# An attention and MLP block: output products over three PSUM banks, scale factors made in PSUM, epsilon as an activation's bias

## The chip, the cores and the metric

The kernel runs on one core of a Trainium2 chip. The metric is the device time of one execution in microseconds (us). Before the change it was 2750.64 us, the median of three runs (2748.8 to 2751.75). Five engines run side by side, each through its own list of instructions in order: TensorE (PE in the profile, its weight loads PEld), VectorE (DVE), ScalarE (ACT), GpSimd (POOL) and SyncE (SP), which issues most of the transfers. Work is held back by semaphores, that is by waits for the end of an instruction on another engine or of a transfer.

## The reference

The input `x` has 2048 rows of 576 values. A condition vector gives shifts, gains and gates; 32 query heads share 16 key and value heads of 512 keys each; the MLP is 4608 wide.

```python
mod = (_silu(c) @ w_mod).reshape(c.shape[0], 6, 1, -1)
sa, ca, ga, sb, cb, gb = (mod[:, 0], mod[:, 1], mod[:, 2], mod[:, 3], mod[:, 4], mod[:, 5])
h = _layernorm(x, axis=-1) * (1 + ca) + sa
x = x + ga * _A_ref(h, A_k_cache, A_v_cache, A_wq, A_wo)
h = _layernorm(x, axis=-1) * (1 + cb) + sb
x = x + gb * _B_ref(h, B_w1, B_w3, B_w2)
```

`_A_ref` projects to queries, takes scores against the last 512 cached keys, a softmax, the sum over the values and an output product with `wo` (4096 by 576). `_B_ref` is `(silu(h @ w1) * (h @ w3)) @ w2`.

## The kernel before

**Tiling.** The rows go in four blocks `b` of 512, each of four row tiles `t` of 128. Every matrix is held as a high and a low half in float16, so that a product is three matmuls: high by high, high by low, low by high. The scale factors that make the halves fit are powers of two, worked out on the chip from the largest value of each matrix.

**Slots and steps.** The attention runs in 128 slots, one for each head and row block, each of four steps t = 0 to 3. The order of every engine's work is the order of the program. In a step TensorE does, in this order: at t = 1 four transposes of probabilities into a T bank (`turn`, L548); the scores of tile t (L513, three matmuls of 512 columns); for t < 3 a part of the next slot's query (L440, L444); one call of `attend_out` (L615); and what the lists of tasks hold for that step. At the end of a slot come the twelve matmuls of `values` (L593). VectorE takes the largest score (L517), ScalarE the exponential `p` (L531) and its high half (L563), GpSimd the low half (L568), and SyncE transposes them by DMA into `ptw` (L575).

**Output products.** For two heads (a pair) and one row tile, a unit, the product with `wo` is twelve matmuls of 128 by 288: two heads, three products of halves, two column halves. A unit is two calls of `attend_out`, j = 0 at an even step and j = 1 at the next, odd one, six matmuls each (L463), written by `back` into the two banks of one tile `E`. After the second, VectorE adds the unit, scaled, to `acc` (L623). The first call of pair p is in slot 2p + 4 at t = 2. `lane` alternates between `E` and a second tile `pf` only from slot n = 128 on, when the T banks are given up for it (L1628).

**PSUM.** Eight banks: two named A (queries and values), two S (scores), two in the tile `E`, two T, each of one bank. T holds the turned probabilities, and also the turned rows of `make_h` (L1446, blocks 2 and 3 of the attention's input, read by `modulate`, L261) and of `store_h` (L655, blocks 0 and 1 of the MLP's input), which have five turns m = 0 to 4, one for each 128 columns, at t = m mod 3. `E` serves a few others: columns 400 to 416 of its second bank take the sums of `sum_peaks` (L330), columns 408 to 411 those of the MLP's weights (`in_total`, `out_total`), and the whole tile the gate rows of `mod_rows` (L176) and the first query (L489).

**Scale steps.** `sum_peaks` spreads the largest values of a weight group over all partitions by a small matmul (L333); `take_sums` (L335) copies them to SBUF (L338); at a later step `scales` (L349) turns them into powers of two by `powers` (L315: L318, L319 and a reciprocal, L320) and for queries and keys into three pairs of factors (`score_factors`, L342, with L345). Queries, keys and values come four to a step (columns 0 to 4), the output's one alone (column 4). `total` tasks run inside `attend_out`, ahead of the accumulation, `taken` tasks behind it, and the step's other tasks after these.

**Norm.** `norm_root` (L210) adds epsilon on VectorE (L213 or L215) and takes the root on ScalarE (L216).

**Start.** The first block's rows are turned into T, T, A, A and S banks, the first query goes to the first bank of `E` (`project_first`, L447 to L456), and `make_h(1)` runs in the first two slots with `early`.

Of the kernel before, what the change touches and what calls it, by code (L numbers as in the profile page):

```python
# [48 lines left out]
def tile_block(  # L49
# [30 lines left out]

    E = psum.tile([P, 2, 512], F32, tag="E", name="pe", bufs=1)
    turning = ExitStack()
    tpool = turning.enter_context(tc.tile_pool(name="tpool", bufs=2, space=PSUM))

    def t_bank():
        return tpool.tile([P, 512], F32, tag="T", name="pt")

# [73 lines left out]
    def mod_cols(wm, name, one, tag):  # L161

        ps = t_bank() if tag == "T" else bank(tag, f"ps_{name}")
# [12 lines left out]
    def mod_rows(wm, kind):  # L176

        vec = gate_rows[kind]
        wm = wm[0]
        for h in range(2):  # L180
            for d in (0, 3):
                nc.tensor.matmul(
                    E[:, h, :HALF], ones, wm[:, d, h * HALF : (h + 1) * HALF], start=d == 0, stop=d == 3
                )
        nc.vector.tensor_copy(half_split(vec), E[:, :, :HALF])
        return vec
# [23 lines left out]
    def norm_root(b):  # L210
        rstd = norms[b][0][:, :, 1]
        if ("out", b) in norms:
            nc.vector.tensor_scalar(rstd, rstd, 1.0 / D, EPS, op0=ALU.mult, op1=ALU.add)  # L213
        else:
            nc.vector.tensor_scalar(rstd, rstd, EPS, None, op0=ALU.add)  # L215
        nc.scalar.activation(rstd, rstd, AF.Sqrt)  # L216

# [36 lines left out]
    def turn_rows(b, m, tag):  # L254

        ps = t_bank() if tag == "T" else bank(tag, "ps_n")
        for t in range(ST):
            nc.tensor.transpose(ps[:, t * P : (t + 1) * P], norms[b][1][t][:, m * P : (m + 1) * P], ident)  # L258
        return ps
# [70 lines left out]
    def sum_peaks(g, lo, hi, ps=None):  # L330

        ps = E[:, 1, 400:416] if ps is None else ps
        nc.tensor.matmul(ps[:, lo:hi], peak_ones, tops[g][:, lo:hi], start=True, stop=True)  # L333

    def take_sums(g, lo, hi, ps=None):  # L335

        ps = E[:, 1, 400:416] if ps is None else ps
        nc.vector.tensor_copy(peaks[g][:, 5 + lo : 5 + hi], ps[:, lo:hi])  # L338

    def score_factors(g):  # L340
        for at_, small, by in (
            (0, peaks[g][:, 5:10], score_down), (3, peaks[g][:, 5:10], turned_down),  # L342
            (5, peaks[g][:, 10:15], log_up),
        ):
            nc.vector.tensor_scalar(  # L345
                factors[:, g, at_ : at_ + 2], small[:, 0:2], small[:, 2:3], by, op0=ALU.mult, op1=ALU.mult
            )

    def scales(g, lo, hi):  # L349

        small = peaks[g]
        powers(small, small[:, 5:10], lo, hi, 5, 2.0**-14)
        down = small[:, 5:10]
        if lo == 0:
            score_factors(g)
        elif lo == 4:
            nc.vector.tensor_scalar(
                factors[:, g, 2:3], down[:, 4:5], down[:, 3:4], gate_down, op0=ALU.mult, op1=ALU.mult
            )
# [97 lines left out]

    def back(ps, o, w, t, first, last):

        rows = slice(t * P, (t + 1) * P)  # L460
        for n, (x, y) in enumerate(((0, 0), (0, 1), (1, 0))):
            for h in range(2):
                nc.tensor.matmul(  # L463
                    ps[:, h, :HALF],
                    o[:, x, rows],
                    w[:, y, h * HALF : (h + 1) * HALF],
                    start=first and n == 0,
                    stop=last and n == 2,
                )

    QP = (range(0, 5), range(5, 10), range(10, 14))
# [13 lines left out]
    def query(i, part):  # L485
        u, j, b = slots[i]
        st = state[i]
        if part == 0 or i == 0:
            st["q"] = bank("A", "pq") if i else E[:, 0, :]  # L489
        ps = st["q"]  # L490
        if i == 0:
            project_first(ps, wqs[u, j], hT[b])
        else:
            project(ps, wqs[u, j], hT[b], QP[part])
        if part == len(QP) - 1:
            q = st["qT"] = pool.tile([P, 2, SB], F16, tag=("qh", "ql")[i % 2], name="qT", bufs=QB)
            nc.scalar.activation(q[:, 0], ps, AF.Copy, scale=Q_DOWN)
            if not i:
                query_low(i)
# [48 lines left out]
    def turn(i, t):  # L548

        st = state[i]  # L550
        p = st.pop(("p", t))
        ps = st["t"] = t_bank().rearrange("p (j n) -> p j n", j=KC)
        for j in range(KC):
# [60 lines left out]

    def attend_out(pair, t, j, total):  # L615
        u, _, b = slots[2 * pair]
        lane[0] += j == 0
        ps = spare()
        back(ps, state[2 * pair + j]["o"], wos[u][:, j], t, j == 0, j == 1)
        if j == 1:  # L620
            run(*total)
            a = half_split(acc[b][:, t, :])
            nc.vector.scalar_tensor_tensor(  # L623
                a, ps[:, :, :HALF], factors[:, uses[u][0], 2:3], a, op0=ALU.mult, op1=ALU.add
            )
# [29 lines left out]
    def store_h(b, m, tag, tag_out):  # L655
# [8 lines left out]
        )  # L664
        store_later(hd[b][m * P : m * P + n, :], hf[:n], ("s", b, m) if tag == "T" else None)

# [266 lines left out]
    def down(d, u):  # L933

        pair = d // G
        lane[0] += 1
        ps = lane[1][lane[0] % 2]
        if u < 4:
# [28 lines left out]
    def plain(j, i, t):  # L967

        d = 2 * G - 1
        lane[0] += 1  # L970
        ps = lane[1][lane[0] % 2]
        w = osets[d, 3 if j else 4]
# [181 lines left out]

    lane = [0, ()]

    def spare():
        return lane[1][lane[0] % 2] if lane[1] else E

    def in_peak(f, part):  # L1160
# [8 lines left out]
    def in_total(f):  # L1169

        m = peak_cols[:, 4 * (f % 2) :][:, :4]
        for part in range(2):
            peak = m[:, 2 * part + 1 : 2 * part + 2]
            nc.tensor.matmul(
                spare()[:, 1, 408:410], peak.to_broadcast([P, P]), m[:, 2 * part : 2 * part + 2],
                start=part == 0, stop=part == 1,
            )

    def in_taken(f):
        nc.vector.tensor_copy(stats[:, f, :], spare()[:, 1, 408:410])  # L1180

# [23 lines left out]
    def out_total(p):  # L1205
        nc.tensor.matmul(spare()[:, 1, 410:411], peak_ones, peak_cols[:, 8 + p % 2 : 9 + p % 2], start=True, stop=True)

    def out_taken(p):
        nc.vector.tensor_copy(out_down[:, p : p + 1], spare()[:, 1, 410:411])

# [235 lines left out]
    def make_h(b, m, early=False):  # L1446
        modulate(hT[b], m, turn_rows(b, m, "T"), vecs["shift", "a"], vecs["gain", "a"], early)

# [33 lines left out]
    for b, i in ((0, 111), (1, 114)):  # L1482
        norm(i, b)
        for m in range(DC + 1):
            at(i + 1 + m // 3, m % 3, store_h, b, m, "T", "raw")
            step_at(ST * (i + 1 + m // 3) + m % 3 + 1, store_now, ("s", b, m))
# [43 lines left out]
    for i, k in ((13, 5), (105, 3), (108, 4)):  # L1530
        at(i - 1, -1, load, wms, k, load_mod, k)
        for d in range(DC + 1):
            at(i, min(d, ST - 1), weigh, k, d)
    at(14, 1, make_gate, "b", 5)
    at(14, 2, lambda: scale_gate("b", mlp_small, mlp_gate_down))
    at(106, 2, make_cols, "shift", "b", 3, 0.0, "T")
    at(109, 2, make_cols, "gain", "b", 4, 1.0, "T")
    at(109, 3, lambda: spread_peaks("b", mlp_small))
    at(110, 1, lambda: scale_cols("b", t_bank(), mlp_small, 2.0**-8))
    for piece in range(6):  # L1540
# [21 lines left out]
    for t in (0, 2, 1, 3):  # L1562
        norm_rows(0, t)
    turned = [turn_rows(0, m, "TTAAS"[m]) for m in range(DC + 1)]
    for m in range(DC + 1):
        weigh_col(wms[0], 0, m, m < 2)
    for k, key in enumerate((wqs[0, 0], wqs[0, 1], keys[0])):
        find_peak(0, k, key)
    sum_peaks(0, 0, 3)
    junk = bank("S", "ps_warm")  # L1570
    warm(junk, WARM[0])
    take_sums(0, 0, 3)
    powers(peaks[0], peaks[0][:, 5:10], 0, 3, 5, 2.0**-14)
    raws = [wqs[0, j] for j in range(2)]
# [12 lines left out]
    modulate_first(hT[0], turned, vecs["shift", "a"], vecs["gain", "a"])  # L1587
    score_factors(0)
    keys[0] = split_k_low(*keys[0], 0)
# [143 lines left out]
```

## Time and profile before

| | |
|---|---|
| time, median of three runs | 2750.64 us |
| lowest and highest | 2748.80, 2751.75 us |
| the profiled execution | 2750.74 us |
| its span, first to last instruction | 2748.9 us |
| TensorE busy | 2678.7 us, 97% |
| VectorE busy | 1943.0 us, 71% |
| ScalarE busy | 1622.0 us, 59% |
| GpSimd busy | 1874.0 us, 68% |
| moved by DMA | 463.87 MB, 169 GB/s |

The page gives busy time per engine; a group row gives an operation's line, the tiles it writes and reads, its count, its busy time and mean, and then the idle time of its engine just before it with what ended that. A row of the timeline is a start in microseconds, a duration, the engine and line, and in square brackets the idle time ahead of it and what ended it. A row of waits reads: engine, tile, line, what it waited for; the sum in microseconds, how often, and the longest. A row of one source line gives the shortest, the middle and the longest duration in ns. Attention fills the span to about 1616 us, the MLP the rest.

### The profile page before, as it was taken

The page shows a single profiled execution, that of the slowest core. Times are in us where ns is not written, and L with a number is a line of the kernel's source. Part 1 is how long each engine was busy: PE and PEld are TensorE (multiplying, and loading weights), DVE is VectorE, ACT ScalarE, POOL GpSimd, SP SyncE. Part 2 cuts the span into 40 slices and gives each one's busy share as a digit, 9 for nine tenths or more (in the row PEclk, how much of TensorE's full clock was granted, in tenths as well). Part 3 has the DMA queues.
Part 4 walks back from the last instruction along what each step waited for, and adds up shares of the span by engine and source line. Part 5 has one row for each costly group of instructions (what it writes and reads, how often), then busy time and mean ns, then how long its engine had stood idle before and what let it go on. Part 6 is the DMA issues. An engine that isn't in the chain of part 4 may idle for free. (4 is left out here: it accounts for less than half of the span.)

```text
span 2748.9 us, 45218 instructions
## 1 busy us (share of the span) xinstructions
PE 2678.7 (97%) x15406; PEld 1510.3 (55%) x15406; DVE 1943.0 (71%) x3582; ACT 1622.0 (59%) x3026; POOL 1874.0 (68%) x1747
## 2 busy tenths in 40 slices
PE   6899999999999999999999999999999999999998
PEld 3455555555555555555555555555555555555555
DVE  7876777777777777877765567777776666566566
ACT  6776778777777778787677635544443333333332
POOL 4677888888888877877669536688874455333435
PEclk9999999999999999999999999999999999999999
DMA  6888888788787878879879945656643444333332
GB/s 200 184 175 196 184 182 186 176 188 187 167 181 170 190 186 211 200 179 212 187 192 226 224 137 169 201 168 200 209 151 111 153 122 128 106 102 112 104 109 81
DMA packets 593463, 463.87 MB, mean 169 GB/s; under 512 B 442704, under 2 KB 472528, under 8 KB 592208
## 3 DMA queue, kind: packets, MB, share of 16 engines
q1 hardware_dynamic: 592944, 460.69, 66.1%
q8 instruction: 121, 1.98, 0.3%
q14 instruction: 110, 0.90, 0.1%
q10 hardware_dynamic: 288, 0.30, 0.0%
HBM read 264.19 MB, written 95.99 MB: 131 GB/s over the span
## 5 line engine op out<-in xcount | busy, mean ns | idle before, releaser
L568 POOL TENSOR_TENSOR hp<-p,hp 128x512 f16<-128x512 f32 x384 | 447.6, 1168 | 267.0 <-ACT hp L563 154.5
L531 ACT ACTIVATE p<-pss,table,factors 128x512 f32<-128x512 f32 x512 | 396.8, 775 | 351.2 <-DVE table L517 182.4
L517 DVE CUSTOM_DVE_ANT_0 spent<-pss,factors 128x512 uint8<-128x512 f32 x512 | 381.2, 745 | 237.6 <-PE pss L513 236.2
L880 PEld LDWEIGHTS <-wset 128*128 128x128 f16 x3528 | 344.2, 98 | 337.2 <-issue 3.7
L880 PE MATMUL py<-hset,wset 128*128 128x512 f16 x2016 | 482.1, 379 | 0.0
L463 PE MATMUL pe<-o 128*128 128x288 f16 x3024 | 453.0, 286 | 10.6 <-DVE acc L623 10.3
L513 PE MATMUL pss<-k,qT 128*128 128x512 f16 x1536 | 417.7, 380 | 15.3 <-ACT p L531 13.0
L463 PEld LDWEIGHTS <-o 128*128 128x128 f16 x3072 | 300.4, 98 | 184.8 <-issue 16.3
L593 PE MATMUL po<-ptw,v 128*128 128x512 f16 x1536 | 357.1, 381 | 8.8 <-DMA ptw<-hp 2.7
L880 PE MATMUL px<-hset,wset 128*128 128x512 f16 x1512 | 361.5, 379 | 2.2 <-ACT p L531 2.2
L94 POOL TENSOR_TENSOR akv<-u,akv 128x512 f16<-128x512 f32 x141 | 165.2, 1181 | 178.0 <-ACT akv L93 170.2
L440 PE MATMUL pq<-hT,wq 128*128 128x512 f16 x1092 | 280.5, 379 | 0.0
L563 ACT CAST hp<-p 128x512 f16<-128x512 f32 x384 | 237.4, 618 | 15.5 <-DMA ptw<-hp 2.3
L593 PEld LDWEIGHTS <-v 128*128 128x128 f16 x1536 | 147.6, 98 | 174.6 <-issue 13.0
L513 PEld LDWEIGHTS <-qT 128*128 128x128 f16 x1536 | 147.3, 98 | 129.3 <-issue 17.4
L965 PEld LDWEIGHTS <-akv 128*128 128x128 f16 x1728 | 169.0, 98 | 89.3 <-issue 0.7
L623 DVE SCALAR_TENSOR_TENSOR acc<-pe,factors,acc 128x576 f32<-128x576 f32 x252 | 204.2, 810 | 13.0 <-PE pe L463 5.1
L613 POOL TENSOR_TENSOR o<-on,o 128x512 f16<-128x512 f32 x128 | 149.7, 1170 | 54.6 <-ACT o L612 52.2
L440 PEld LDWEIGHTS <-wq 128*128 128x128 f16 x1092 | 106.9, 98 | 127.2 <-issue 1.0
L959 DVE SCALAR_TENSOR_TENSOR acc<-pf,table,acc 128x576 f32<-128x576 f32 x140 | 113.5, 811 | 79.3 <-PE pf L965 79.3
L1058 ACT COPY u<-py 128x512 f32<-128x512 f32 x72 | 42.2, 586 | 200.8 <-PE py L880 198.8
L1051 ACT ACTIVATE s<-s,table 128x512 f32<-128x512 f32 x72 | 52.0, 722 | 175.6 <-DVE s L1050 175.6
(254 smaller groups left out, 4734.2 us busy)
## 6 DMA issues: line engine op xcount, KB each, us to landing
wset<-wd SPq DMA_DIRECT2D x213, 320.0 KB, 3.2
r<-row SPq DMA_DIRECT2D x128, 256.0 KB, 3.9
oset<-od SPq DMA_DIRECT2D x106, 288.0 KB, 3.2
wraw<-in_w SPq DMA_DIRECT2D x36, 768.0 KB, 5.4
wd<-wmade SPq DMA_DIRECT2D x75, 320.0 KB, 3.5
wset<-wd SPq DMA_DIRECT2D x71, 160.0 KB, 2.2
w2raw<-in_w SPq DMA_DIRECT2D x19, 576.0 KB, 5.2
wd<-ring SPq DMA_DIRECT2D x33, 320.0 KB, 2.7
```

What stands on the lines that cost most here:

```text
L94: eng.tensor_sub(halves[:, 1], src, halves[:, 0])
L440: nc.tensor.matmul(ps, w[:, k // 2, m, :], hT[:, DC + m if k == 1 else m, :], start=s == 0, stop=False)
L463: nc.tensor.matmul(ps[:, h, :HALF], o[:, x, rows], w[:, y, h * HALF : (h + 1) * HALF], start=first and n == 0, stop=last and n == 2,)
L513: nc.tensor.matmul(pss, q[:, x, rows], k[:, y, :], start=n == 0, stop=n == 2)
L517: nc.vector.tensor_tensor_reduce(spent, pss, to_log.to_broadcast([P, W]), turned, 3.0e38, op0=ALU.add, op1=ALU.min, accum_out=nm)
L531: nc.scalar.activation(p, pss, AF.Exp, bias=nm, scale=factor, accum_out=st["l"][:, t : t + 1])
L563: nc.scalar.copy(hp[:, 0, :], state[i]["p", t])
L568: nc.gpsimd.tensor_sub(hp[:, 1, :], state[i].pop(("p", t)), hp[:, 0, :])
L593: nc.tensor.matmul(po, v[:, x, c, :], pt[:, y, c, :], start=c == 0 and n == 0, stop=c == KC - 1 and n == 2)
L623: nc.vector.scalar_tensor_tensor(a, ps[:, :, :HALF], factors[:, uses[u][0], 2:3], a, op0=ALU.mult, op1=ALU.add)
L880: nc.tensor.matmul(ps, w[:, a, :], h[:, b, :], start=start and n == 0, stop=stop and n == 6, skip_group_check=True)
L965: nc.tensor.matmul(ps[:, h, :HALF], a[:, rows], w[:, b, :], start=m == 0, stop=m == 2)
```

## The change

`E` becomes one tile of three banks, in the pool that held the T banks, and T has one bank. `lane` flips with every unit: a unit takes the middle bank and one outer bank, first or last. Part 0 (the even step) issues six terms into the outer bank, part 1 (the odd step) the six terms for the middle bank; for t = 0 the last term of part 0 is put off to part 1. `idle()` is the outer bank that the running unit does not use: turned rows, column vectors and gates go there. The sums go to columns 400 and up of the third bank, where `take_sums` now works out the powers in place and copies both columns to SBUF once; `score_factors` reads them there. Epsilon is the bias of the root's activation. `make_gate` "b" and its scaling move one step later. The first sums are taken in an S bank, the first rows are turned into `E[:, 0]` and `E[:, 1]`, the first query goes to `E[:, 2]`, and the early `make_h(1)` alternates between `E[:, 0]` and `E[:, 1]`. At slot n the pool is closed and two tiles of two banks, `pe` and `pf`, are allocated.

```diff
-    E = psum.tile([P, 2, 512], F32, tag="E", name="pe", bufs=1)
-    tpool = turning.enter_context(tc.tile_pool(name="tpool", bufs=2, space=PSUM))
-    def t_bank():
-        return tpool.tile([P, 512], F32, tag="T", name="pt")
+    tpool = turning.enter_context(tc.tile_pool(name="tpool", bufs=1, space=PSUM))
+    E = tpool.tile([P, 3, 512], F32, tag="E", name="pe")
+    lane = [1, ()]
+    def both_halves():
+        banks = lane[1][lane[0]] if lane[1] else E[:, lane[0] : lane[0] + 2]
+        return banks[:, :, :HALF]
+    def idle():
+        return E[:, 2 - 2 * lane[0], :]
+    def spare():
+        return lane[1][lane[0]][:, 1] if lane[1] else E[:, 2]
...
-        if ("out", b) in norms:
-            nc.vector.tensor_scalar(rstd, rstd, 1.0 / D, EPS, op0=ALU.mult, op1=ALU.add)
-        else:
-            nc.vector.tensor_scalar(rstd, rstd, EPS, None, op0=ALU.add)
-        nc.scalar.activation(rstd, rstd, AF.Sqrt)
+        nc.scalar.activation(rstd, rstd, AF.Sqrt, bias=eps_col, scale=1.0 / D if ("out", b) in norms else 1.0)
...
-        ps = t_bank() if tag == "T" else bank(tag, "ps_n")
+        ps = idle() if tag == "E" else E[:, int(tag), :] if tag in "012" else bank(tag, "ps_n")
...
-        nc.vector.tensor_copy(peaks[g][:, 5 + lo : 5 + hi], ps[:, lo:hi])
+        both = ps[:, :10].rearrange("p (k n) -> p k n", n=5)[:, :, lo:hi]
+        d, up = both[:, 0], both[:, 1]
+        nc.vector.tensor_scalar(d.bitcast(I32), d.bitcast(I32), EXPONENT, None, op0=ALU.bitwise_and)
+        nc.vector.tensor_scalar(d, d, 2.0**-40, 2.0**-14, op0=ALU.max, op1=ALU.mult)
+        nc.vector.reciprocal(up, d)
+        nc.vector.tensor_copy(peaks[g][:, 5:15].rearrange("p (k n) -> p k n", n=5)[:, :, lo:hi], both)
+    def score_factors(g, ps=None):
+        ps = E[:, 2, 400:416] if ps is None else ps
+        for at_, k, by in ((0, 0, score_down), (3, 0, turned_down), (5, 5, log_up)):
             nc.vector.tensor_scalar(
-                factors[:, g, at_ : at_ + 2], small[:, 0:2], small[:, 2:3], by, op0=ALU.mult, op1=ALU.mult
+                factors[:, g, at_ : at_ + 2], ps[:, k : k + 2], peaks[g][:, k + 7 : k + 8], by,
+                op0=ALU.mult, op1=ALU.mult,
...
     def scales(g, lo, hi):
-        small = peaks[g]
-        powers(small, small[:, 5:10], lo, hi, 5, 2.0**-14)
-        down = small[:, 5:10]
+        down = peaks[g][:, 5:10]
...
-            st["q"] = bank("A", "pq") if i else E[:, 0, :]
+            st["q"] = bank("A", "pq") if i else E[:, 2, :]
...
-        ps = st["t"] = t_bank().rearrange("p (j n) -> p j n", j=KC)
+        ps = st["t"] = tpool.tile([P, KC, P], F32, tag="T", name="pt")
...
-    def attend_out(pair, t, j, total):
-        lane[0] += j == 0
-        ps = spare()
-        back(ps, state[2 * pair + j]["o"], wos[u][:, j], t, j == 0, j == 1)
-        if j == 1:
+    TERMS = tuple((j, x, y) for j in range(2) for x, y in ((0, 0), (0, 1), (1, 0)))
+    def attend_out(pair, t, part, total):
+        if not part:
+            lane[0] = 1 - lane[0]
+        now, last = lane[0], [(lane[0], TERMS[-1])] if t == 0 else []
+        if part:
+            jobs = last + [(1 - now, term) for term in TERMS]
+        else:
+            jobs = [(now, term) for term in TERMS[: len(TERMS) - len(last)]]
+        for h, (j, x, y) in jobs:
+            nc.tensor.matmul(
+                both_halves()[:, h],
+                state[2 * pair + j]["o"][:, x, t * P : (t + 1) * P],
+                wos[u][:, j, y, h * HALF : (h + 1) * HALF],
+                start=(j, x, y) == TERMS[0],
+                stop=(j, x, y) == TERMS[-1],
+            )
+        if part:
...
-    at(14, 1, make_gate, "b", 5)
-    at(14, 2, lambda: scale_gate("b", mlp_small, mlp_gate_down))
+    at(14, 2, make_gate, "b", 5)
+    at(14, 3, lambda: scale_gate("b", mlp_small, mlp_gate_down))
...
-    at(110, 1, lambda: scale_cols("b", t_bank(), mlp_small, 2.0**-8))
+    at(110, 1, lambda: scale_cols("b", idle(), mlp_small, 2.0**-8))
...
-    turned = [turn_rows(0, m, "TTAAS"[m]) for m in range(DC + 1)]
+    turned = [turn_rows(0, m, "01AAS"[m]) for m in range(DC + 1)]
...
-                    lane[1] = (E, after.tile([P, 2, 512], F32, tag="T2", name="pf"))
+                    lane[1] = tuple(after.tile([P, 2, 512], F32, tag=tag, name=tag) for tag in ("pe", "pf"))
```

More of the change, by code (lines that the diff above doesn't have):

```diff
@@ L142, in tile_block @@
     ones = ones.to_broadcast([P, P])
+    eps_col = const.tile([P, 1], F32, name="eps_col")
+    nc.gpsimd.memset(eps_col, EPS)
     peak_cols = const.tile([P, 12], BF16, name="peak_cols")
@@ L161, in mod_cols @@
     def mod_cols(wm, name, one, tag):
-        ps = t_bank() if tag == "T" else bank(tag, f"ps_{name}")
+        ps = idle() if tag == "E" else bank(tag, f"ps_{name}")
         wm = wm[0]
@@ L179, in mod_rows @@
         wm = wm[0]
+        ps = E[:, 1 - lane[0] : 3 - lane[0], :HALF]
         for h in range(2):
@@ L182, in mod_rows @@
                 nc.tensor.matmul(
-                    E[:, h, :HALF], ones, wm[:, d, h * HALF : (h + 1) * HALF], start=d == 0, stop=d == 3
+                    ps[:, h], ones, wm[:, d, h * HALF : (h + 1) * HALF], start=d == 0, stop=d == 3
                 )
-        nc.vector.tensor_copy(half_split(vec), E[:, :, :HALF])
+        nc.vector.tensor_copy(half_split(vec), ps)
         return vec
@@ L330, in sum_peaks @@
     def sum_peaks(g, lo, hi, ps=None):
-        ps = E[:, 1, 400:416] if ps is None else ps
+        ps = E[:, 2, 400:416] if ps is None else ps
         nc.tensor.matmul(ps[:, lo:hi], peak_ones, tops[g][:, lo:hi], start=True, stop=True)
     def take_sums(g, lo, hi, ps=None):
[L337 to L344, printed above, removed]
+        ps = E[:, 2, 400:416] if ps is None else ps
+        both = ps[:, :10].rearrange("p (k n) -> p k n", n=5)[:, :, lo:hi]
[5 more added lines that the diff above has]
+    def score_factors(g, ps=None):
+        ps = E[:, 2, 400:416] if ps is None else ps
+        for at_, k, by in ((0, 0, score_down), (3, 0, turned_down), (5, 5, log_up)):
             nc.vector.tensor_scalar(
-                factors[:, g, at_ : at_ + 2], small[:, 0:2], small[:, 2:3], by, op0=ALU.mult, op1=ALU.mult
+                factors[:, g, at_ : at_ + 2], ps[:, k : k + 2], peaks[g][:, k + 7 : k + 8], by,
+                op0=ALU.mult, op1=ALU.mult,
             )
     def scales(g, lo, hi):
-        small = peaks[g]
-        powers(small, small[:, 5:10], lo, hi, 5, 2.0**-14)
-        down = small[:, 5:10]
+        down = peaks[g][:, 5:10]
         if lo == 0:
@@ L456, in project_first @@
                     nc.tensor.matmul(ps, w[:, k, DC, :], hT[:, 2 * DC, :], start=False, stop=False)
[L458 to L469, printed above, removed]
     QP = (range(0, 5), range(5, 10), range(10, 14))
@@ L623, in attend_out @@
             nc.vector.scalar_tensor_tensor(
-                a, ps[:, :, :HALF], factors[:, uses[u][0], 2:3], a, op0=ALU.mult, op1=ALU.add
+                a, both_halves(), factors[:, uses[u][0], 2:3], a, op0=ALU.mult, op1=ALU.add
             )
@@ L664, in store_h @@
         )
-        store_later(hd[b][m * P : m * P + n, :], hf[:n], ("s", b, m) if tag == "T" else None)
+        store_later(hd[b][m * P : m * P + n, :], hf[:n], ("s", b, m) if tag == "E" else None)
     def combine_tiles(pair):
@@ L935, in down @@
         pair = d // G
-        lane[0] += 1
-        ps = lane[1][lane[0] % 2]
+        lane[0] = 1 - lane[0]
+        ps = lane[1][lane[0]]
         if u < 4:
@@ L969, in plain @@
         d = 2 * G - 1
-        lane[0] += 1
-        ps = lane[1][lane[0] % 2]
+        lane[0] = 1 - lane[0]
+        ps = lane[1][lane[0]]
         w = osets[d, 3 if j else 4]
@@ L1153, in tile_block @@
     nc.gpsimd.memset(odd_cols, 1.0)
-    lane = [0, ()]
-    def spare():
-        return lane[1][lane[0] % 2] if lane[1] else E
     def in_peak(f, part):
@@ L1174, in in_total @@
             nc.tensor.matmul(
-                spare()[:, 1, 408:410], peak.to_broadcast([P, P]), m[:, 2 * part : 2 * part + 2],
+                spare()[:, 412:414], peak.to_broadcast([P, P]), m[:, 2 * part : 2 * part + 2],
                 start=part == 0, stop=part == 1,
@@ L1179, in in_taken @@
     def in_taken(f):
-        nc.vector.tensor_copy(stats[:, f, :], spare()[:, 1, 408:410])
+        nc.vector.tensor_copy(stats[:, f, :], spare()[:, 412:414])
     def power_of(up, d, down):
@@ L1205, in out_total @@
     def out_total(p):
-        nc.tensor.matmul(spare()[:, 1, 410:411], peak_ones, peak_cols[:, 8 + p % 2 : 9 + p % 2], start=True, stop=True)
+        nc.tensor.matmul(spare()[:, 414:415], peak_ones, peak_cols[:, 8 + p % 2 : 9 + p % 2], start=True, stop=True)
     def out_taken(p):
-        nc.vector.tensor_copy(out_down[:, p : p + 1], spare()[:, 1, 410:411])
+        nc.vector.tensor_copy(out_down[:, p : p + 1], spare()[:, 414:415])
     def out_scale(p):
@@ L1446, in make_h @@
     def make_h(b, m, early=False):
-        modulate(hT[b], m, turn_rows(b, m, "T"), vecs["shift", "a"], vecs["gain", "a"], early)
+        modulate(hT[b], m, turn_rows(b, m, str(m % 2) if early else "E"), vecs["shift", "a"], vecs["gain", "a"], early)
     def statistics(i, b, steps):
@@ L1484, in tile_block @@
         for m in range(DC + 1):
-            at(i + 1 + m // 3, m % 3, store_h, b, m, "T", "raw")
+            at(i + 1 + m // 3, m % 3, store_h, b, m, "E", "raw")
             step_at(ST * (i + 1 + m // 3) + m % 3 + 1, store_now, ("s", b, m))
@@ L1533, in tile_block @@
             at(i, min(d, ST - 1), weigh, k, d)
-    at(14, 1, make_gate, "b", 5)
-    at(14, 2, lambda: scale_gate("b", mlp_small, mlp_gate_down))
-    at(106, 2, make_cols, "shift", "b", 3, 0.0, "T")
-    at(109, 2, make_cols, "gain", "b", 4, 1.0, "T")
+    at(14, 2, make_gate, "b", 5)
+    at(14, 3, lambda: scale_gate("b", mlp_small, mlp_gate_down))
+    at(106, 2, make_cols, "shift", "b", 3, 0.0, "E")
+    at(109, 2, make_cols, "gain", "b", 4, 1.0, "E")
     at(109, 3, lambda: spread_peaks("b", mlp_small))
-    at(110, 1, lambda: scale_cols("b", t_bank(), mlp_small, 2.0**-8))
+    at(110, 1, lambda: scale_cols("b", idle(), mlp_small, 2.0**-8))
     for piece in range(6):
@@ L1568, in tile_block @@
         find_peak(0, k, key)
-    sum_peaks(0, 0, 3)
     junk = bank("S", "ps_warm")
+    first_sums = junk[:, 400:416]
+    sum_peaks(0, 0, 3, first_sums)
     warm(junk, WARM[0])
-    take_sums(0, 0, 3)
-    powers(peaks[0], peaks[0][:, 5:10], 0, 3, 5, 2.0**-14)
+    take_sums(0, 0, 3, first_sums)
     raws = [wqs[0, j] for j in range(2)]
@@ L1587, in tile_block @@
     modulate_first(hT[0], turned, vecs["shift", "a"], vecs["gain", "a"])
-    score_factors(0)
+    score_factors(0, first_sums)
     keys[0] = split_k_low(*keys[0], 0)
```

## The prediction

> **What bounds the kernel.** I read the head of the page, the cores view, the groups of instructions by line on TensorE, then its waits by releaser.
>
> ```profile
> PE 2678.7 (97%) x15406; PEld 1510.3 (55%) x15406; DVE 1943.0 (71%) x3582; ACT 1622.0 (59%) x3026; POOL 1874.0 (68%) x1747
> core 0: 2748.9 us, clock 0.997
> L463 PE MATMUL pe<-o 128*128 128x288 f16 x3024 | 453.0, 286 | 10.6 <-DVE acc L623 10.3 <-DVE us L338 0.2
> L513 PE MATMUL pss<-k,qT 128*128 128x512 f16 x1536 | 417.7, 380 | 15.3 <-ACT p L531 13.0 <-ACT qT L497 0.9 <-DVE qT L503 0.5
> PE pss L513 <- ACT p L531: 13.0, 17, 2.4
> PE pe L463 <- DVE acc L623: 10.3, 14, 2.0
> ```
>
> TensorE is busy 97% of the span at a granted clock of 0.997, and its order is fixed, so time moves only where TensorE itself waits. 2748.9 − 2678.7 leaves 70 us of idle time in all; the two waits above, 23.3 us, are those at which the change is near. The sum is made against the profiled execution, 2750.74 us (span 2748.9 and 1.8 around it); the median of the runs, 2750.64, is the same to 0.1. A measurement tells about 0.2%, 5.5 us, from no change.
>
> The output products keep their 12 matmuls a unit, and their order is free of cost: 453.0 us over 3024 is 150 ns each, whichever bank comes next. So the change is priced in waits alone.
>
> **What it removes: long scale operations.** The factor steps are tiny VectorE operations on SBUF.
>
> ```profile
> L319 DVE TENSOR_SCALAR us<-us x35: 153/155/1349, 16.1 to 1259.8; 128x1 f32<-128x1 f32 x19, 128x4 f32<-128x4 f32 x15, 128x3 f32<-128x3 f32 x1
> L345 DVE TENSOR_SCALAR factors<-us,sc x48: 257/282/1448, 29.3 to 1216.3; 128x2 f32<-128x2 f32 x48
> L338 DVE COPY us<-pe x33: 145/151/161, 14.8 to 1255.3; 128x1 f32<-128x1 f32 x17, 128x4 f32<-128x4 f32 x15, 128x3 f32<-128x3 f32 x1
> L345 DVE TENSOR_SCALAR factors<-us,sc 128x2 f32<-128x2 f32 x48 | 23.4, 546 | 0.0
> L319 DVE TENSOR_SCALAR us<-us 128x1 f32<-128x1 f32 (+2 forms) x35 | 14.8, 423 | 1.2
> L318 DVE TENSOR_SCALAR us<-us 128x1 int32<-128x1 int32 (+2 forms) x35 | 9.3, 266 | 0.5
> 400.81 1.40 POOL L846 TENSOR_TENSOR w2raw<-w2raw,gate_b 128x576 f32<-128x576 f32 x1
> 400.89 1.35 DVE L319 TENSOR_SCALAR us<-us 128x4 f32<-128x4 f32 x1
> 402.17 1.16 POOL L568 TENSOR_TENSOR hp<-p,hp 128x512 f16<-128x512 f32 x1
> 402.37 0.98 DVE L345 TENSOR_SCALAR factors<-us,sc 128x2 f32<-128x2 f32 x1
> 407.49 0.81 PE L513 MATMUL pss<-k,qT 128*128 128x512 f16 x3 [1.05 <-ACT p L531]
> 410.40 0.81 PE L513 MATMUL pss<-k,qT 128*128 128x512 f16 x3 [0.45 <-ACT p L531]
> 313.69 0.81 PE L513 MATMUL pss<-k,qT 128*128 128x512 f16 x3 [1.21 <-ACT p L531]
> 115.52 0.90 PE L463 MATMUL pe<-o 128*128 128x288 f16 x6 [0.30 <-DVE acc L623]
> 599.43 0.77 PE L463 MATMUL pe<-o 128*128 128x288 f16 x5 [0.29 <-DVE acc L623]
> ```
>
> At 400.89 a 155 ns operation takes 1349 ns and ends at 402.24, when GpSimd's L846 ends (402.21). Over the mean-minus-shortest of each group, 48 × 0.289 + 35 × 0.270 + 35 × 0.13 is 28 us of VectorE time lost beside GpSimd. L338, the one with its source in PSUM, never exceeds 161 ns. [...]
>
> What that is worth is not 28 us but what TensorE later waits: 6 to 10 us behind each such step, ScalarE is late with `p` and scores wait (407.49: 1.05, 410.40: 0.45; 313.69: 1.21). Followed step by step over the 12 late score factors from 109 to 1166 us, with 0.1 to 0.2 us more of restart per wait than the idle figure shows, these give 11.2 us; the wait total of L513 on p, 13.0, less three in the first 90 us, bounds it above with the accumulator waits of the same steps (115.5: 0.3, 599.4: 0.3). The dropped value-factor operations add 0.5. Gain **11.7** (bounds 8 and 14).
>
> ```profile
> 8.49 0.17 DVE L215 TENSOR_SCALAR mv<-mv 128x4 f32<-128x4 f32 x1
> 214.60 1.72 PE L182 MATMUL pe<-wm,ones 128*128 128x288 f32 x6 [0.91 <-DVE acc L623]
> ```
>
> Epsilon as a bias removes L215; only the first, 0.17 us at 8.49, lies ahead of TensorE's first work: gain 0.2. `make_gate` "b" moves from t = 1, behind a running accumulation, to t = 2, where none runs: its 0.91 (1.07 with the restart) falls away, and part 1 of that unit waits about 0.3 for its copy: gain 0.8. Together the gains are **12.7 us**.
>
> **What it adds: waits of the one tile.** Does TensorE, writing one bank of E, wait for readers of another?
>
> ```profile
> 730.54 0.15 DVE L338 COPY us<-pe 128x1 f32<-128x1 f32 x1
> 730.74 0.77 PE L463 MATMUL pe<-o 128*128 128x288 f16 x5 [0.21 <-DVE us L338]
> PE pe L463 <- DVE us L338: 0.2, 1, 0.2
> ```
>
> The first matmul at 730.74 writes bank 0 (`h` 0); L338 reads columns 400 to 416 of bank 1. It waits all the same, to 0.05 us after the copy. So E is ordered as a whole, and the change keeps E one tile, of three banks. Two things follow. Part 0 of a unit still waits for the accumulation of the last one although its own bank is free: the 10.3 us of L463 on acc stay, but for the 0.6 counted above. And what used to go to the two T banks, the transposes of `make_h` and `store_h`, now waits for whatever reads E.
>
> ```profile
> 138.89 0.90 PE L463 MATMUL pe<-o 128*128 128x288 f16 x6
> 139.62 0.60 PE L258 MATMUL pt<-ident,xn 128*128 128x128 f32 x4
> 139.82 0.82 DVE L623 SCALAR_TENSOR_TENSOR acc<-pe,factors,acc 128x576 f32<-128x576 f32 x1
> 140.06 0.81 PE L513 MATMUL pss<-k,qT 128*128 128x512 f16 x3
> 143.39 0.90 PE L463 MATMUL pe<-o 128*128 128x288 f16 x6
> 144.18 0.77 ACT L273 ACTIVATE hf<-pt,mod_a 128x512 f32<-128x512 f32 x1
> ```
>
> Terms, each a delay of TensorE, with all its queue behind the waiting instruction:
> - Transposes at t = 1 (m = 1 and 4 of two `make_h` and two `store_h` blocks: eight) come right behind part 1. They start at 139.62; the accumulation ends at 140.64. 140.64 + 0.06 − 139.62 = 1.08; eight are 8.6. One of them also stands behind a value sum (0.7), and one lets the next part 0 wait (0.3): **9.7**. Scores are queued behind it, and VectorE and ScalarE behind those, which had little ahead; nothing hides it.
> - Transposes at t = 2 (m = 2, four) are read by ScalarE's modulation, 144.95 its end, while part 1 wants E at 143.39: 1.56, and 1.4 to 2.2 at the other three. TensorE is already 1.08 late there in part, so I take **4.1** (3.1 to 7.4). Those at t = 0 leave part 1 some 0.1 to 1 us behind their read: nothing.
> - `scale_cols` in the idle bank, one more wait for an accumulation: **1.1**.
>
> ```profile
> 102.89 0.14 DVE L338 COPY us<-pe 128x1 f32<-128x1 f32 x1
> 103.45 0.78 PE L463 MATMUL pe<-o 128*128 128x288 f16 x5
> ```
>
> - `take_sums` becomes four operations in PSUM. For a single value sum it stands at t = 1, and part 0 comes 103.45 − 103.03 = 0.42 after the copy. Three more operations at 0.15 to 0.2 start to start (400.50 to 400.69 to 400.89) are 0.6: 0.2 late at each of 15: **3.2** (0 to 7, if such operations in PSUM take 0.1 or 0.3). At the fours (t = 3) seven operations, 1.35 us, face 0.9 to 2.0 of room: **0.9**.
>
> ```profile
> 23.61 2.12 PE L450 MATMUL pe<-hT,wq 128*128 128x512 f16 x8 [0.74 <-ACT hT L287]
> 25.45 0.79 ACT L287 ACTIVATE hf<-pt,mod_a 128x512 f32<-128x512 f32 x1
> 28.91 0.92 PE L453 MATMUL pe<-hT,wq 128*128 128x512 f16 x3 [0.76 <-POOL hT L296]
> 38.43 0.63 PE L258 MATMUL pt<-ident,xn 128*128 128x128 f32 x4 [0.79 <-DVE hT L269]
> 41.80 1.11 PE L258 MATMUL pt<-ident,xn 128*128 128x128 f32 x4 [2.74 <-ACT hT L271]
> ```
>
> - Prologue. The first rows turned stand in E, and the first query too: it must wait for the last read of them, 26.24, in place of 23.61. The end of that query hangs on GpSimd's low part (28.91) in any case, so of 2.6 I take 0.9 (0 to 2.4). The early `make_h(1)` had two T banks in turn; in E its five turns go one after another with their reads: the third, at 41.80, moves to about 44.15, **+2.3**. Prologue **3.2** (0.5 to 6).
>
> Costed at nothing: the single bank for T's `turn`, used once a step, its copies out done a step ahead; part 0 now needs the second head's `o` a step earlier, and has 4 us of room; the pool renewed at slot n; no DMA is moved.
>
> **Sum:** 9.7 + 4.1 + 1.1 + 3.2 + 0.9 + 3.2 = 22.2 lost, 12.7 gained, **+9.5: 2760 us**. With the upper and lower ends of the unsure terms, its own range is 2750 to 2770.
>
> **Rivals.**
> - **E is ordered bank by bank (faster).** Place: part 0's first matmul, and the t = 1 transposes. If only readers of the same bank hold TensorE, the outer bank is free while VectorE adds up the last unit, and the idle bank while it is read.
>
> ```profile
> 1535.18 0.90 PE L463 MATMUL pe<-o 128*128 128x288 f16 x6 [1.99 <-DVE acc L623]
> ```
>
>   Such waits as 1535.18 then go: of the 10.3 some 5 find nothing else late behind them, and with the slower matmuls that follow 1535 and the restarts 8.4. The locks bring 11.2, gate and epsilon 0.6 or more; the idle bank still costs 3.4 where its read comes into part 0, and the chains 1. 2750.7 − 8.4 − 11.2 − 0.6 + 3.4 + 1.0 ≈ **2735**. It decides from the point that a matmul starts in E while the accumulation of the unit before runs. The row at 730.74 speaks against it. [...] Chance 0.12.
> - **The added waits are half hidden (no change).** Time lost at 139 to 192 us may be got back at later waits for GpSimd or DMAs, as TensorE still has 70 us of idle time; then 22 becomes about 12, and the time is **2750**. Against it: those waits are rare between 135 and 300 us. Chance 0.25.
> - **The locks stay, or the reads run at their upper ends (slower still).** Each scale operation also takes a scalar or the copy's target from SBUF; if the long ones remain, 2760 + 11 ≈ **2771**. L338, whose target lies in SBUF, speaks against it. Chance 0.08.
> - **Forecast:** 0.55.
>
> **How the numbers follow.** Likeliest is the forecast, 2760. Leaving out most of the fast rival (0.12) and the top of the slow one, the range is 2743 to 2772. Faster by over 5.5 us: the fast rival and a tail, 0.13. Within 5.5: the hidden case, 0.25. Slower: 0.62.
>
> **What would show it.** Right: L318, L319 and L345's successors all under 0.3 us; the waits of L513 on p down from 13.0 to about 3; L463 on acc still near 10; new waits of the transposes on acc near 1 us, eight times, and of L463 on ScalarE's modulation. Wrong: part 0 starting while the accumulation before it runs, or transposes with no wait at 139 and 1387 us, would mean the fast rival; scale operations over 1 us, the slow one.

## The result and the profile after

The changed kernel takes 2766.16 us (median of 6 runs, 2765.08 to 2774.07) beside 2750.21 us for the kernel before: a ratio of 1.0065, 95% interval 1.0054 to 1.0077, or +16 us. The profiled execution is 2767.13 us long, with a span of 2765.2. The forecast was slower, 2760; the time lies in its range, 2743 to 2772, but 6 us beyond the likeliest value.

The head of the page, the cores view, two groups of instructions by line and TensorE's waits, now with the changed kernel's line numbers (L510 are the scores, L624 the output matmuls, L634 the accumulation, L265 the transposes, L350 the copy of the sums):

```profile
PE 2683.3 (97%) x15406; PEld 1513.0 (55%) x15406; DVE 1918.7 (69%) x3574; ACT 1624.9 (59%) x3026; POOL 1870.6 (68%) x1748
core 0: 2765.2 us, clock 0.994
L624 PE MATMUL pe<-o 128*128 128x288 f16 x3024 | 452.1, 286 | 17.9 <-DVE acc L634 6.3 <-DVE us L350 4.1 <-ACT hf L673 2.7
L510 PE MATMUL pss<-k,qT 128*128 128x512 f16 x1536 | 417.2, 380 | 7.1 <-ACT p L528 5.5 <-ACT qT L494 0.9
PE pe L265 <- DVE xn L246: 11.7, 1, 11.7
PE pe L265 <- DVE acc L634: 6.0, 6, 1.1
PE pe L265 <- ACT hT L278: 4.6, 2, 2.8
```

TensorE's work is the same number of instructions. Scores wait on `p` for 5.5 us where it was 13.0: that part of the change did what it says. The output matmuls wait 17.9 where it was 10.6, and transposes wait for the accumulation, which they never did. (The 11.7 us of the first row is the time before the first transpose.) Set beside each other score by score, the two traces tell where the 16 us come from. How much later a score starts in the changed kernel is called its lag here. The first scores of slot 0 lag by 8.1 us (30.52 to 38.64), those of slot 1, t = 1, by 12.1 (46.24 to 58.38). From slot 7 to slot 13, where two `make_h` run, the lag grows from 13.0 to 21.8. Then it shrinks, to 11.8 at 1186 us (slot 94). From slot 109 to 116, with `store_h` and `scale_cols`, it grows to 21.9; over the last slots of the attention it falls to 17.9, and the end of the MLP is 16.4 late.

Rows of one source line each, the shortest, middle and longest duration in ns: the powers' two operations and the score factors, now with PSUM sources.

```profile
L347 DVE TENSOR_SCALAR pe<-pe x32: 158/168/171, 60.3 to 1267.4; 128x1 int32<-128x1 int32 x17, 128x4 int32<-128x4 int32 x15
L348 DVE TENSOR_SCALAR pe<-pe x32: 166/167/171, 60.5 to 1267.6; 128x1 f32<-128x1 f32 x17, 128x4 f32<-128x4 f32 x15
L356 DVE TENSOR_SCALAR factors<-pe,us,sc x45: 269/271/280, 69.2 to 1227.6; 128x2 f32<-128x2 f32 x45
```

None is long any more: the longest are 171 and 280 ns, where they were 1349 and 1448. With their sources in PSUM the shortest are 12 to 22 ns longer than before (136, 153 and 257 ns).

The timeline around a `make_h` turn, the place that the prediction read at 139 to 144 us:

```profile
151.89 0.90 PE L624 MATMUL pe<-o 128*128 128x288 f16 x6
152.89 0.82 DVE L634 SCALAR_TENSOR_TENSOR acc<-pe,factors,acc 128x576 f32<-128x576 f32 x1
153.77 0.66 PE L265 MATMUL pe<-ident,xn 128*128 128x128 f32 x4 [0.98 <-DVE acc L634]
157.82 0.77 ACT L280 ACTIVATE hf<-pe,mod_a 128x512 f32<-128x512 f32 x1
158.64 1.02 PE L624 MATMUL pe<-o 128*128 128x288 f16 x7 [1.01 <-ACT hf L280]
```

The transposes go to the idle bank, the accumulation reads the two others, and still the transposes start 0.06 us after it ends. Five microseconds later part 1 writes the middle bank and waits for ScalarE's read of the idle one, in which the next turn (t = 2) lies.

The start of the kernel:

```profile
8.72 0.21 DVE L208 BATCH_NORM_AGGREGATE mv<-bst 128x2 f32<-128x12 f32 x1
9.01 1.28 ACT L223 ACT_TABLE_LOAD   x1 [2.51 <-DVE mv L208]
16.42 0.21 PE L340 MATMUL ps_warm<-top,peak_cols 128*128 128x3 bf16 x1
16.49 4.53 PE L231 MATMUL ps_warm<-ident,ones 128*128 128x128 f32 x36
21.05 0.17 DVE L347 TENSOR_SCALAR ps_warm<-ps_warm 128x3 int32<-128x3 int32 x1 [5.62 <-PE ps_warm L231]
26.16 0.79 PE L1132 MATMUL ps_warm<-spread,ones 128*128 128x128 f32 x2 [5.15 <-DVE spread L1131]
32.10 3.57 PE L460 MATMUL pe<-hT,wq 128*128 128x512 f16 x8 [3.12 <-ACT hf L294]
46.31 0.66 PE L265 MATMUL pe<-ident,xn 128*128 128x128 f32 x4 [1.14 <-DVE hT L276]
49.77 1.11 PE L265 MATMUL pe<-ident,xn 128*128 128x128 f32 x4 [2.80 <-ACT hT L278]
52.70 1.12 PE L265 MATMUL pe<-ident,xn 128*128 128x128 f32 x4 [1.82 <-ACT hT L278]
```

Of what stands here the prediction had two things: the wait of the first query (L460) and the early turns, one behind the other (46.31 to 52.70). It did not have the table load at 9.01, behind the statistics, and it did not have the step at 21.05: the first sums now lie in the bank that the 36 warming matmuls write, so VectorE sits still for 5.62 us until they are through. And the eight matmuls of the first query take 3.57 us where they took 2.12 before.

### The profile page after: what moved, and what is told of

Its sections match the earlier page's. It is cut to its first block, busy times and chain, and to the rows that moved or that the text cites. A ratio compares the mean times of both kernels' runs of the same rounds, so it can differ in the third digit from the quotient of the medians.

```text
span 2765.2 us, 45329 instructions
## 1 busy us (share of the span) xinstructions
PE 2683.3 (97%) x15406; PEld 1513.0 (55%) x15406; DVE 1918.7 (69%) x3574; ACT 1624.9 (59%) x3026; POOL 1870.6 (68%) x1748
## 5 line engine op out<-in xcount | busy, mean ns | idle before, releaser
L624 PE MATMUL pe<-o 128*128 128x288 f16 x3024 | 452.1, 286 | 17.9 <-DVE acc L634 6.3
L510 PE MATMUL pss<-k,qT 128*128 128x512 f16 x1536 | 417.2, 380 | 7.1 <-ACT p L528 5.5
L624 PEld LDWEIGHTS <-o 128*128 128x128 f16 x3072 | 300.0, 98 | 193.7 <-issue 28.4
L634 DVE SCALAR_TENSOR_TENSOR acc<-pe,factors,acc 128x576 f32<-128x576 f32 x252 | 204.5, 812 | 18.5 <-PE pe L624 8.9
L510 PEld LDWEIGHTS <-qT 128*128 128x128 f16 x1536 | 147.4, 98 | 117.0 <-issue 8.7
L970 DVE SCALAR_TENSOR_TENSOR acc<-pe,table,acc 128x576 f32<-128x576 f32 x140 | 113.6, 811 | 79.6 <-PE pe L976 79.6
```

The costliest lines, as they stand in the source:

```text
L510: nc.tensor.matmul(pss, q[:, x, rows], k[:, y, :], start=n == 0, stop=n == 2)
L624: nc.tensor.matmul(both_halves()[:, h], state[2 * pair + j]["o"][:, x, t * P : (t + 1) * P], wos[u][:, j, y, h * HALF : (h + 1) * HALF], s ...
L634: nc.vector.scalar_tensor_tensor(a, both_halves(), factors[:, uses[u][0], 2:3], a, op0=ALU.mult, op1=ALU.add)
```

## The experiments

Theory: TensorE waits for every reader of E because E is one tile; the start adds waits of its own; relief of the scale operations is real and worth about what was forecast. The rivals stand with each run. Ratios are to the kernel before, run beside it, with 95% intervals.

**E as three tiles.** Each bank is a tile, and the accumulation is one operation a bank, two for a unit. The copy of the gate rows is split in the same way.

```diff
-    E = tpool.tile([P, 3, 512], F32, tag="E", name="pe")
+    E = [tpool.tile([P, 512], F32, tag=f"E{k}", name=f"pe{k}") for k in range(3)]
...
+                for h in (now, 1 - now):
+                    nc.vector.scalar_tensor_tensor(
+                        a[:, h], half_bank(h), factors[:, uses[u][0], 2:3], a[:, h], op0=ALU.mult, op1=ALU.add
+                    )
```

> The changed kernel with E as three tiles of one bank each; the accumulation of a unit is two VectorE operations, one a bank. Theory (TensorE waits for every reader of E because E is one tile): the waits of transposes and output matmuls on acc and on ScalarE's hf go, some 16 us in slots 8 to 13 and 112 to 116, about 6 of part 0 on acc, half of the 5 behind sums, and some 4 to 5 at the start (query and early make_h): 2735 us (2728 to 2745). Rival (the waits are real lateness of VectorE, or of one bank): no change or a loss by 250 more VectorE operations, 2764 to 2772.

Measured: 2748.65 us, ratio 0.9998 (0.9989 to 1.0008). So 17.5 us come back, not 31. The timeline of the same place and the waits of this kernel:

```profile
145.03 0.90 PE L624 MATMUL pe<-o 128*128 128x288 f16 x6
145.74 0.92 DVE L640 SCALAR_TENSOR_TENSOR acc<-pe,factors,acc 128x288 f32<-128x288 f32 x2
145.76 0.60 PE L265 MATMUL pe<-ident,xn 128*128 128x128 f32 x4
```

```profile
PE po L590 <- DVE ptw L580: 7.0, 15, 0.7
PE px L897 <- ACT p L528: 3.4, 1, 3.4
PE pe L624 <- DVE factors L356: 2.4, 7, 0.5
PE pe L624 <- ACT hf L280: 1.4, 2, 1.2
PE pe L624 <- DVE acc L640: 1.3, 2, 1.1
```

The transposes at 145.76 start while the accumulation runs: the wait was the tile's, not the bank's. The lag hardly grows any more where two `make_h` run (6.1 us at the start of slot 8, 7.9 at slot 13, beside 13.0 and 21.8 in the changed kernel), and the waits on the accumulation fall from 6.3 and 6.0 to 1.3 and nothing. But waits for `ptw` rise from 2.9 to 7.0. Two things could be behind the missing 13 us: what the start still has, and VectorE's two operations. A third stands in the trace: at the start of slot 127 this execution is 18.6 us ahead of the changed kernel, at the end 14.5, and between them lies the wait for `p` at L897, 3.4 us here and 1.4 there.

**The same two operations, one tile.**

```diff
-            nc.vector.scalar_tensor_tensor(
-                a, both_halves(), factors[:, uses[u][0], 2:3], a, op0=ALU.mult, op1=ALU.add
-            )
+            for h in (now, 1 - now):
+                nc.vector.scalar_tensor_tensor(
+                    a[:, h], both_halves()[:, h], factors[:, uses[u][0], 2:3], a[:, h], op0=ALU.mult, op1=ALU.add
+                )
```

> The changed kernel, E still one tile, with the accumulation as two operations, one a bank. Theory (splitting E missed its 2735 by the 0.2 us that two operations take more, 250 times, on VectorE, which shows as waits for ptw and for factors): 2766 plus 4 to 12, since part 0 also waits 0.2 us longer where it waits: 2773 us (2769 to 2780). Rival (the extra work of VectorE is covered; splitting E simply brought less): 2765 to 2768.

Measured: 2776.47 us, ratio 1.0095 (1.008 to 1.0111), 10.3 more than the changed kernel. The source rows of the accumulation, one operation in the changed kernel and two here:

```profile
L634 DVE SCALAR_TENSOR_TENSOR acc<-pe,factors,acc x252: 779/809/820, 105.9 to 1630.1; 128x576 f32<-128x576 f32 x126
```

```profile
L635 DVE SCALAR_TENSOR_TENSOR acc<-pe,factors,acc x504: 480/508/520, 105.0 to 1640.7; 128x288 f32<-128x288 f32 x168
```

Two at 508 ns are 207 ns more than one at 809; over 252 units, 52 us of VectorE time, of which 10 come out in the kernel's time. So splitting E is probably worth more than the 17.5 us that it shows. An estimate is 28, the two figures added; that the two operations cost the same 10 us where E is split was not measured.

**The first sums in a bank of their own.**

```diff
-    first_sums = junk[:, 400:416]
+    first_sums = tpool.tile([P, KC, P], F32, tag="T", name="pt")[:, 0, :16]
```

> The changed kernel with the first sums in a T bank instead of the S bank that the warming matmuls write. Theory (VectorE's first scale step waits for 36 warming matmuls because they write the same bank): that step starts at about 16.6 instead of 21.1 us, and the first scores come 4.5 to 7 us earlier: 2760 us (2757 to 2763). Rival (the start is late through the activation table or GpSimd's low halves, the wait is covered): under 1 us, 2765 to 2767.

Measured: 2767.6 us (4 runs, 2763.35 to 2768.97), ratio 1.0066 (1.0051 to 1.0081): no gain in the total. The timeline of its start:

```profile
15.62 0.17 DVE L347 TENSOR_SCALAR pt<-pt 128x3 int32<-128x3 int32 x1 [0.99 <-PE pt L340]
21.40 0.49 PE L1132 MATMUL ps_warm<-spread,ones 128*128 128x128 f32 x2 [1.73 <-DVE spread L1131]
33.79 1.11 PE L510 MATMUL pss<-k,qT 128*128 128x512 f16 x3 [0.69 <-ACT qT L494]
```

The step starts at 15.62 and the first scores at 33.79, 4.85 us earlier than in the changed kernel, as the theory said. Score by score, 4.0 us of it are left at the end of slot 5, 1.9 at the end of slot 124, and at the end of the kernel this execution is 1.8 behind. Much of the loss falls at the end of the attention: the wait for `p` before a run of MLP matmuls is 2.18 where the changed kernel has 1.38, and the mean granted clock from 1594 to 1600 us is 0.72 where the changed kernel has 1.00.

```profile
1594.28 1.99 PE L891 MATMUL px<-hset,wset 128*128 128x512 f16 x7 [2.18 <-ACT p L528]
1594.00:1600.00 6.00, 5.72 (x22) 2.66 (x22) 0.99 (x2) 2.72 (x7) 1.90 (x2) 0.72 1.05 325
```

(The second row is the windows view: the stretch, its length, busy time of the five engines, the granted clock, DMA share, GB/s.) TensorE comes there 1.9 us earlier than in the changed kernel, but `p` is ready only 1.1 us earlier (the matmuls start at 1594.28 and 1595.41), so part of the lead is waited away. What holds `p` back was not followed further. An early gain is not a gain at the end.

**Epsilon back on VectorE.** `norm_root` as before, the rest as changed.

> The changed kernel with epsilon added on VectorE as before. Theory (with a second operand to wait for, the load of the root's table moves from 6.4 us, beside idle time, to 9.0, behind the statistics): first transposes 1.3 to 1.6 us earlier, 2764.7 us (2763.5 to 2766). Rival (the first rows just arrived later in that run): 2766 or 0.2 more.

Measured: 2765.68 us, ratio 1.0061 (1.0046 to 1.0076); beside the changed kernel's 2766.16 the total can't tell. The timeline can:

```profile
5.99 1.28 ACT L225 ACT_TABLE_LOAD   x1
8.19 0.21 DVE L206 BATCH_NORM_AGGREGATE mv<-bst 128x2 f32<-128x12 f32 x1
9.89 2.41 PE L267 MATMUL pe<-ident,xn 128*128 128x128 f32 x8 [9.89 <-DVE xn L248]
```

The table load is back at 5.99, beside idle time. That it went behind the statistics because the root has a second operand to wait for fits, but the run shows only that it goes with the bias. From the end of the last statistics to the first transpose it is 9.89 − 8.40 = 1.49 us, and 11.65 − 8.93 = 2.72 in the changed kernel, a difference that does not hang on when the rows arrive: 1.2 us.

**The scale factors alone.** The kernel before, E and T as they were, with the powers of all sums and the score factors (but for those of the first group) made in PSUM, and other columns for the MLP's sums.

```diff
+        both = ps[:, :10].rearrange("p (k n) -> p k n", n=5)[:, :, lo:hi]
+        d, up = both[:, 0], both[:, 1]
...
+        nc.vector.tensor_copy(peaks[g][:, 5:15].rearrange("p (k n) -> p k n", n=5)[:, :, lo:hi], both)
...
-                factors[:, g, at_ : at_ + 2], small[:, 0:2], small[:, 2:3], by, op0=ALU.mult, op1=ALU.mult
+                factors[:, g, at_ : at_ + 2], ps[:, k : k + 2], peaks[g][:, k + 7 : k + 8], by,
+                op0=ALU.mult, op1=ALU.mult,
```

> The kernel before with the powers and score factors of all weight groups but the first worked out in PSUM (the second bank of its E, other columns for the MLP's sums). Theory (lock relief is worth 11.7 us, the longer chain of sums costs 4 to 6 of it): scale operations all under 0.3 us, 2744 us (2739 to 2748). Rival (the long operations were covered, only the chain remains): 2751 to 2756.

Measured: 2741.14 us, ratio 0.9972 (0.996 to 0.9985). The relief is real: 9.0 us beside the 2750.14 of the kernel before in these runs, with the longer chain against it.

**Only the fours in PSUM.** The same, but a single sum is copied at once and its powers are made in SBUF two steps later.

```diff
+        if lo == 4:
+            nc.vector.tensor_copy(peaks[g][:, 9:10], ps[:, 4:5])
+            return
```

> The kernel before with the powers and score factors worked out in PSUM only where four (or the first three) sums come together; a single output sum is copied at once and its powers are made in SBUF two steps later, as before. Theory (the factor steps of the fours hold the long operations; the longer chain of the ones only delays part 0, 0.38 us at each of 13): 4 to 5 us better than with all sums in PSUM, 2736.5 us (2733 to 2740). Rival (those 0.38 are caught up later, or the ones' operations in SBUF become long): 2740 to 2744.

Measured: 2739.63 us (5 runs, 2734.63 to 2744.5), ratio 0.9962 (0.9949 to 0.9974): the lowest median of the study, 26.5 us below the changed kernel. Score by score it gains 0.37 to 0.38 us on the kernel above at slots 33, 49, 65, 81, 85, 89, 93, 97 and 101, where a single sum stands, as the theory has it; but the two medians lie only 1.5 us apart, and their intervals overlap, so the gain in the total is not shown. The single sums' steps, back in SBUF, do not become long: the longest of their 18 multiplications takes 155 ns. Waits of TensorE in the two kernels, all sums in PSUM first:

```profile
PE pe L466 <- DVE us L343: 3.1, 12, 0.8
```

```profile
PE pe L471 <- DVE us L339: 1.4, 1, 1.4
```

Eleven of the twelve waits go, all but one of them 0.2 us long. At the first place, now at 102.79, the wait is longer instead, behind a copy that comes late.

**Both mended, three tiles and one.** The changed kernel with first sums apart, single sums as before and epsilon on VectorE, once with E split and once with E whole.

> The changed kernel with E as three tiles, the first sums in a T bank, single sums as before and epsilon on VectorE. Theory (these are separate waits, each with its own price): 4.8 for the first sums, about 3 for the ones, 1.3 for the table: 2739.5 us (2736 to 2744). Rival (VectorE's added work bounds the attention whatever is taken off): 2744 to 2749.

> The changed kernel, E one tile of three banks and one accumulation, with the first sums in a T bank, single sums as before and epsilon on VectorE: what is left of the change's cost is E as one tile. Theory (E as one tile costs the waits of transposes and of part 1, and the start's; about 15 us beside the kernel before with the fours in PSUM): 2766 less 4.8, 4.9 and 1.3: 2755 us (2751 to 2759). Rival (with the start and the single sums mended the rest is caught up): 2745 or less.

Measured: split 2741.84 us, ratio 0.9972 (0.996 to 0.9983); whole 2759.56 (2753.25 to 2762.73), ratio 1.0038 (1.0025 to 1.0051). The two differ in E alone, and by 17.7 us, with VectorE's added work counted in. The waits of the whole one, from its fastest execution (2753.25 us):

```profile
PE pe L631 <- DVE acc L641: 7.4, 9, 2.0
PE pe L267 <- DVE acc L641: 6.0, 6, 1.1
PE pe L267 <- ACT hT L280: 4.6, 2, 2.8
PE pe L467 <- ACT hf L296: 4.1, 1, 4.1
PE pe L631 <- ACT hf L680: 2.7, 2, 1.7
```

These are the waits that the split removes. The whole one came 4.5 us above its expectation: three mends of 11 us in sum brought 6.6, and the start's share, which did not last in the run with the first sums apart, may be the reason; that was not tested by itself.

## Why the prediction was right, and by how much off

**E is ordered as a whole: right.** The row at 730.74 said so, and the two last runs show that one tile in place of three costs 17.7 us, more than the whole loss of 16. The fast rival, E by banks, is the split kernel in all but the form of the accumulation. That kernel gets the waits away, but it measured no faster than the kernel before (ratio 0.9998); with the 10.3 us of the second operation taken off, an estimate, it would stand at 2738, near the rival's 2735. The split kernel, guarded by bank, starts its transposes at 145.76, 0.02 us after the accumulation's start; the whole tile is a stricter guard that the program put there, and in the changed kernel TensorE waits 0.98 us for it at 153.77.

**Transposes and modulation: right in mechanism, a little small at 9.7, 4.1 and 1.1, 14.9 in sum.** The lag grows by 8.8 us from slot 7 to slot 13 and by 8.6 from slot 109 to 116, 17.4 in all, with some tenths that come back between; 1.1 of it is a wait for a DMA at 215.82 that no term had. All eight transposes at t = 1 wait, six of them for the accumulation by the waits view. The wait is 0.98 idle in most, and the scores behind it start 1.20 later, for 1.08 forecast; the one behind a value sum costs 2.0. The eight add 10.5 to the lag, part 1's four waits for the modulation (0.7 to 1.7 idle, 1.01 at 158.64) add 5.4, and `scale_cols` 1.2.

**Relief of the long scale operations (the prediction's "locks"): right.** That a source in PSUM would keep them short was the author's estimate from L338, never over 161 ns. Forecast 11.7 and, with single sums against it, 8.5 or so. The slow rival, in which the long operations stay, is out: none is over 280 ns. In the changed kernel the lag falls by 9.2 from slot 15 to slot 94 (21.0 to 11.8); alone, in the kernel before, it brings 9.0, and 9.6 without the single sums (2749.2 to 2739.63). Scores still wait 5.5 us on `p`, where about 3 was forecast. With PSUM sources not one of 109 operations (L347, L348, L356) is long; why a source in PSUM shortens them was not shown.

**Single sums: right in kind, forecast at about half their size.** 0.38 us each, for 0.2 forecast: the copy ends at 116.21 and L624 starts at 116.27; the operations in PSUM take 168 ns, not 155, and follow each other by 0.2.

**The fours and the gate: right.** Part 0 waits once for the longer chain at t = 3 and part 1 once for the gate's copy, 0.5 and 0.2 us idle, for 0.9 and 0.3 forecast. One sign came otherwise: output matmuls wait 6.3 us for the accumulation, where the prediction let 10 stay.

```profile
PE pe L624 <- DVE factors L356: 0.5, 1, 0.5
PE pe L624 <- DVE gate_b L196: 0.2, 1, 0.2
```

**The start: the step that failed.** The prologue, forecast at 3.2 (0.5 to 6), measured 12.1, twice the upper bound. Three things were missing or had the wrong sign. First, the sums moved into the S bank of the warming matmuls. The sum has no term for it, but VectorE's step now comes behind 36 matmuls (4.9 us at the first scores, shown by the sums apart). Second, epsilon as a bias, priced as a gain of 0.2, is a loss: the root's table load went behind the statistics, and the load's 1.28 us come onto the path (1.2 us, shown). Third, the clock falls behind the waits so made, of which the prediction's prologue says nothing: in the windows view of the changed kernel the clock (the third number from the end) is 0.50 from 26 to 32 us and from 49 to 58; in the kernel before it is 1.00 at the first query.

```profile
26.00:32.00 6.00, 2.44 (x8) 1.88 (x9) 4.95 (x13) 5.40 (x12) 4.49 (x8) 0.50 0.31 100
49.00:58.00 9.00, 6.42 (x21) 3.83 (x22) 3.77 (x7) 3.75 (x6) 3.84 (x4) 0.50 0.22 55
```

```profile
23.00:30.00 7.00, 3.78 (x14) 1.25 (x13) 6.93 (x11) 6.44 (x13) 5.70 (x5) 1.00 0.62 207
```

**What came back.** Of the 9 us too few at the start, some 4 were made up from slot 116 to the end of the attention (21.9 to 17.9) and 1.6 in the MLP; the sum had neither. That the total is only 6 us off is partly such a balance, and so luck. Of the hidden rival, in which some half of the loss comes back, this much came true: 5.5 us of the 21.9. The traces show where it came back: the kernel before waits at three places late in the attention for VectorE or ScalarE, and the changed kernel, coming later, waits less there or not at all. At 1535.18 the kernel before waits 1.99 us, and a stretch at half clock follows (0.50 from 1536.21 to 1539.62); the changed kernel waits 1.43 at full clock (1.00 from 1554 to 1560), and 2.25 us of the lag go. At 1574.57 it waits 1.29, the changed kernel not at all. The next wait is 2.18, and 1.38 in the changed kernel. From the kernel before and, last, the changed one:

```profile
1574.57 0.90 PE L463 MATMUL pe<-o 128*128 128x288 f16 x6 [1.29 <-DVE acc L623]
1578.29 1.67 PE L880 MATMUL px<-hset,wset 128*128 128x512 f16 x7 [2.18 <-ACT p L531]
1556.24 0.77 PE L624 MATMUL pe<-o 128*128 128x288 f16 x5 [1.43 <-DVE acc L634]
```

No run was made to test this.

## What to carry to other kernels

In this program a tile is the unit of waiting as much as of memory (the transposes at 153.77 waited 0.98 us for a read of other banks): banks that are meant to be used by different engines at once belong to different tiles, and the cost of an operation that then has to be split is to be weighed (0.2 us a unit here, 10 us in all with E whole, beside 17.5 that the split brings with this cost in it). The small VectorE steps that grew long beside GpSimd were cured by a source in PSUM (the longest 171 and 280 ns, for 1349 and 1448); a longer chain there had its price where TensorE waited for the bank (0.38 us at each single sum). Here that cure alone gave 0.3 to 0.4%, and the rest of the change took it away and more. Moving a small result into "a free corner" of a bank can put it behind whatever else writes that bank, as the first sums came behind the warming matmuls (VectorE idle for 5.62 us).

## What the runs showed of the hardware

TensorE's granted clock had a mean of 0.997 in the kernel before and 0.994 in the changed one; it stood at 1.00 but for stretches at 0.50, and a wait's length alone did not tell whether one followed. From 85 us on, those left out that the kernel's end cuts off, the kernel before has two such stretches, from 1536.21 to 1539.62 and from 2734.29 to 2737.70, and the changed kernel one, from 92.14 to 95.55: 3.41 us each. Ahead of 1536.21 lies a wait of 1.99 us (ended at 1535.18), ahead of 2734.29 two of 0.75 and 1.22 (ended at 2732.05 and 2734.16), and ahead of 92.14 most of the first of these two, both from the changed kernel:

```profile
92.27 1.44 PE L510 MATMUL pss<-k,qT 128*128 128x512 f16 x3 [2.40 <-ACT p L528]
1595.41 1.67 PE L891 MATMUL px<-hset,wset 128*128 128x512 f16 x7 [1.38 <-ACT p L528]
```

Three score matmuls that take 0.81 us elsewhere take 1.44 after the first wait, and seven take the usual time, 1.67, after the second. The sharper pair was shown above: 2.18 us in the kernel before (1578.29), and 2.18 with the first sums apart (1594.28). After the first the seven matmuls take 1.67 us and the clock is 1.00 from 1577.17 to 1582; after the second they take 1.99, and the mean clock from 1594 to 1600 us is 0.72. What decides between two such waits was not shown.
